# 46 products of 32 by 32 ahead of the first output transposes, in a DeltaNet and hard-swish MLP kernel

## The chip, the cores and the metric

The kernel runs on one core of one Trainium2 chip. The core has five engines that work in parallel, each through its own instruction stream in order: TensorE (PE in the profile; its weight loads are PEld), VectorE (DVE), ScalarE (ACT), GpSimd (POOL) and SyncE (SP), which here issues the DMA transfers. Engines wait for each other through semaphores. The metric is the device time of one execution in microseconds (us), lower is better. The kernel before has a median of 660.53 us over three runs (659.67 to 660.70).

## The reference

Two blocks follow each other. The first is a delta-rule recurrence over 768 tokens for 4 batches and 8 heads of width 48; the second is an MLP from 384 to 2048 and back with a hard-swish, over the 3072 tokens of all batches.

```python
def _attn_ref(q, k, v, beta):            # q, k, v: (4, 8, 768, 48); beta: (4, 8, 768)
    k_n = k / (np.linalg.norm(k, axis=-1, keepdims=True) + 1e-06)
    state = np.zeros((B, H, D, D), dtype=np.float32)
    for t in range(S):
        kt, vt, bt = (k_n[:, :, t], v[:, :, t], beta[:, :, t, None])
        y[:, :, t] = np.einsum('bhd,bhde->bhe', q[:, :, t], state)
        v_old = np.einsum('bhde,bhd->bhe', state, kt)
        state = state + bt[:, :, :, None] * np.einsum('bhd,bhe->bhde', kt, vt - v_old)
    return y

def _moe_ref(x, w_in, w_out):            # x: y as (3072, 384)
    h = x @ w_in
    g = h * np.clip(h + 3.0, 0.0, 6.0) / 6.0
    return g @ w_out
```

## The kernel before

The recurrence is worked in 24 steps of 32 tokens. A step holds the 32 tokens of all 4 batches on 128 partitions, batch b on rows 32b to 32b + 31, and all 8 heads beside each other. Within a step the 32 tokens depend on each other through a lower triangular matrix for each batch and head; its inverse, X, is made ahead of the step. Step 0 and groups of up to four steps have their own ways to X: step 0 by products (L645), group 1 (steps 1 to 4) by `halves_of`, an elimination of two halves on VectorE (transpose into the tile A at L458, pairs of multiply and subtract at L779 and L784, transpose back to X at L462), joined for each step by `join` (VectorE transposes at L743 and L751, TensorE products at L733).

The function `chain(t)` then does step t: products of keys and queries with the state (ks, L854, from step 1 on), the right side R, Z = X R (pz, L875), the change of the state (su, L986; subtracted at L1004), and, in `output`, the step's result: LB times Z (py, L875), copied to the tile y (L909 for step 0, on ScalarE), three transposes of 128 by 128 against the identity into the PSUM tile yt (L921), and a ScalarE copy of yt into xT (L925). xT is the input of the MLP. `prep` makes the transposed keys and queries (pt, L570) and the scores (sc, L596).

The MLP takes two steps, 256 tokens, as a block; there are 12 blocks. For block 0 the up product runs on each half of the block separately. `up` (L1042) writes a PSUM tile ph for each of 16 columns of tiles f, in three products of 128 by 128 by 128; ScalarE makes a first g from ph (L1049), VectorE finishes it from g and ph (L1052), and only then is the PSUM tile free. Four PSUM slots, named pm, are handed round by the function `ring` between pt, pz, py, yt, ph and others. `down` is L1210; later blocks use other schemes for both products (L1114 and L1274).

Weights come in pieces of 768 KB (L320) and are converted: four powers on ScalarE (L345) and three operations on VectorE (L367, L372, L378) for each piece.

The order of each engine's instructions is the order in which the program emits them. For the first five steps this is written out in the string ORDER, a list of short words; after them a plan emits steps and MLP units in turn. In ORDER the word y0 emits the pieces of step 0's `output` one after the other, ua the columns f of the first half block, i1 the elimination for group 1, a and c the conversion of the weights. So on TensorE the order at this place is: the transposes and scores of later steps, py of step 0, the three transposes yt, ph for f = 0, 1, 2, ks of step 1, ph for f = 3 to 9, the first pi of `join` for step 1, ph for f = 10, the second pi, and so on. On ScalarE it is: four powers of a piece of weights, the copy of y, the copy to xT, the first g of f = 0 and 1, three powers, the first g of f = 2, 3 and 4. On VectorE the elimination of group 1 stands between the conversion of weights and the g's of f = 0 to 5, and the transpose to X follows.

A product of f32 operands is two passes on TensorE, each with its weight load, so that 32 products show as 64 matmuls in the profile. A transpose is one pass.

Of the kernel before, what the change touches and what calls it, by code (L numbers as in the profile page):

```python
# [44 lines left out]
def kernel(  # L45
# [21 lines left out]
    nc = tc.nc  # L67
    B, H, S, D = q.shape
    DM, FF = moe_w_in.shape
    C, DP = 32, 64  # L70
# [24 lines left out]
    def rows(b):  # L95
        return slice(C * b, C * b + C)
# [4 lines left out]
    def group(t):  # L101
        return (0, t) if t < G0 else ((t - G0) // GS + 1, (t - G0) % GS)
# [34 lines left out]
    def needs(*what):  # L137
        assert past.issuperset(what), (what, set(what) - past)
# [5 lines left out]
    def ring(tag, n, key):  # L144

        held = rings.setdefault(tag, [])
        i = len(held)
        if i < n:
            held.append(key)
        else:  # L150
            i = min(range(n), key=lambda i: reads.get(held[i], len(reads)))
            needs(("read", held[i]))
            held[i] = key
        slot[tag] = f"{tag}{i}"

    def read(*keys):
        for key in keys:
            past.add(("read", key))
            reads.setdefault(key, len(reads))
# [45 lines left out]
    ident = const.tile([128, 128], FP32, name="ident")  # L205
# [623 lines left out]
    def he(h):  # L829
        return (h % 2) * NP + h // 2  # L830

    def by_pair(t):
        return t.rearrange("p (a e w) -> p e a w", e=2, w=D)

    def chain(t, whole=True):


# [27 lines left out]
        def plus(out, ph, sign, into):  # L865
            for e in range(2):
                nc.vector.scalar_tensor_tensor(
                    out=by_pair(out)[:, e], in0=ph[:, e], scalar=sign, in1=by_pair(into)[:, e],
                    op0=ALU.mult, op1=ALU.add,
                )  # L870

        def of_heads(ps, place, m, z, at=lambda h: h):
            for h in range(H):
                for b in range(B):
                    nc.tensor.matmul(  # L875
                        ps[rows(place(b)), D * h : D * h + D],
                        lhsT=m(h)[rows(b)], rhs=z[rows(b), D * at(h) : D * at(h) + D],
                        start=True, stop=True, skip_group_check=True,
                        tile_position=(C * b, C * place(b)),
                    )  # L880
# [4 lines left out]
        def output(Z=None):  # L885

            if t > 0:
                needs(("turned", t - 1))
            y = work.tile([P, DM], FP32, name="y", bufs=1)
            if t > 0:  # L890
                nc.scalar.activation(
                    out=by_pair(y[:]), in_=even, func=ACTF.Copy, scale=parity[:, 1, 1:2]
                )
                past.add(("even", t))
                if ("R", t) in past:
                    read(("ks", t, 0))
                yield 1
                plus(y[:], odd, parity[:, 0, 1:2], y[:])
                read(*(("ks", t, i) for i in range(2)))
                yield  # L900
            needs(("Z", t))
            Z = zs.pop(t)
            ring("pm", NPM, ("py", t))
            py = psM.tile([P, 512], FP32, name="py", tag=slot["pm"])
            of_heads(py, lambda b: b ^ 1, lambda h: LB[:, he(h), :], Z)
            past.add(("BZ", t))
            yield
            if t == 0:
                nc.scalar.activation(out=y[:], in_=py[:, 0:DM], func=ACTF.Copy)  # L909
            else:  # L910
                nc.vector.tensor_tensor(out=y[:], in0=y[:], in1=py[:, 0:DM], op=ALU.add)
            read(("py", t))
            yield
            blk, cc = divmod(t, CB)
            if cc == 0:
                needs(*([("up", blk - 2)] if blk >= 2 else []))
                xTs[blk] = work.tile([128, NKT, TB], FP32, name="xT")
            ring("pm", NPM, ("yt", t))
            pt = psM.tile([128, NKT, P], FP32, name="yt", tag=slot["pm"])
            for s in range(NKT):  # L920
                nc.tensor.transpose(pt[:, s, :], y[:, s * 128 : (s + 1) * 128], ident[:])  # L921
            past.add(("turned", t))
            yield 1
            read(("yt", t))
            nc.scalar.activation(  # L925
                out=xTs[blk][:, :, cc * P : (cc + 1) * P], in_=pt[:], func=ACTF.Copy
            )
            past.add(("seam", t))
            yield

        outs[t] = output()
        even = odd = None
        if t > 0:
# [475 lines left out]
    def chain_of(t):  # L1409
        return made(("h", t), lambda: chain(t))  # L1410
# [39 lines left out]
    def early_norms(t):  # L1450
# [9 lines left out]
    )  # L1460
    makers = {
        "p": lambda t: prep(t, False), "h": lambda t: chain(t, False), "y": lambda t: outs[t],
        "n": early_norms, "m": mask, "b": scaled, "x": lambda t: product(t) if t < G0 else join(t),
        }
# [35 lines left out]
    with tc.manual_schedule():  # L1500
# [16 lines left out]
        for t in range(LS, N):  # L1517
            g, i = group(t)
# [118 lines left out]
```

## Time and profile before

| | |
|---|---|
| median of three runs | 660.53 us |
| profiled execution | 661.58 us |
| its span, first to last instruction | 659.9 us |
| mean granted TensorE clock over the span | 0.984 |
| TensorE idle before the yt of step 0, ended by the copy of y | 1.18 us |
| TensorE matmul passes | 11640 |
| TensorE idle from 73.55 us to the end, in waits | none listed |

The median is of runs of the kernel as it is; the profiled execution is one run more, and its span leaves out what lies ahead of the first and behind the last instruction (1.7 us). Times in the views count from the first instruction of the span. The granted clock is 1 for full speed and 0.5 for half. In the order of time of an engine, a row is start, length, engine, line, operation, names and count of like instructions in a row; in brackets stands how long the engine was idle before it and what released it. "issue" there means that the profile shows nothing that it waited for.

### The profile page before, as it was taken

The page shows a single profiled execution, that of the slowest core. Times are in us where ns is not written, and L with a number is a line of the kernel's source. Part 1 is how long each engine was busy: PE and PEld are TensorE (multiplying, and loading weights), DVE is VectorE, ACT ScalarE, POOL GpSimd, SP SyncE. Part 2 cuts the span into 40 slices and gives each one's busy share as a digit, 9 for nine tenths or more (in the row PEclk, how much of TensorE's full clock was granted, in tenths as well). Part 3 has the DMA queues.
Part 4 walks back from the last instruction along what each step waited for, and adds up shares of the span by engine and source line. Part 5 has one row for each costly group of instructions (what it writes and reads, how often), then busy time and mean ns, then how long its engine had stood idle before and what let it go on. Part 6 is the DMA issues. An engine that isn't in the chain of part 4 may idle for free.

```text
span 659.9 us, 26616 instructions
## 1 busy us (share of the span) xinstructions
PE 630.5 (96%) x11640; PEld 567.1 (86%) x11640; DVE 504.9 (77%) x1164; ACT 264.3 (40%) x553; POOL 230.5 (35%) x352
## 2 busy tenths in 40 slices
PE   2759999999999999999999999999999999999997
PEld 2648887776689999999999999999999999999997
DVE  5989777799558989758989858989658999456354
ACT  4876578322232154154144244244243144153240
POOL 6531033002653262564163462263251241231330
PEclk9768999999999999999999999999999999999999
DMA  7888246402041030041030040030020020000101
GB/s 173 206 209 228 68 101 152 69 17 49 12 83 23 2 74 4 2 80 33 3 74 3 3 75 2 2 62 3 3 49 3 4 48 3 23 18 2 26 1 24
DMA packets 88693, 33.29 MB, mean 50 GB/s; under 512 B 80224, under 2 KB 83424, under 8 KB 88576
## 3 DMA queue, kind: packets, MB, share of 16 engines
q1 hardware_dynamic: 88224, 31.29, 21.8%
q8 instruction: 91, 1.49, 1.0%
q10 hardware_dynamic: 352, 0.30, 0.2%
q14 instruction: 26, 0.21, 0.1%
HBM read 26.84 MB, written 4.72 MB: 48 GB/s over the span
## 4 chain that ended last, share of the span: by engine, by line
PE 90%; DMA 3%; DVE 3%; SPq 1%; ACT 1%; issue 1%; DVEq 0%; ACTq 0%
PE po L1274 28%; PE ph L1114 27%; PE ph L1042 9%; PE po L1210 6%; PE pz L875 3%; PE py L875 3%; PE pc L854 3%; PE pt L570 2%; PE pc L986 2%; DMA spare<-in_moe_w_in_dram 2%; PE pc L596 1%; PE yt L921 1%; PE sc L596 1%; PE ks L854 1%; SPq L168 1%
## 5 line engine op out<-in xcount | busy, mean ns | idle before, releaser
L1114 PE MATMUL ph<-xT,w_in 128*128 128x128 f32 (+1 forms) x720 | 154.3, 320 | 0.0
L1078 POOL TENSOR_TENSOR g<-g 128x256 f32<-128x256 f32 (+1 forms) x144 | 89.7, 624 | 97.0 <-ACT g L1128 91.3
L1114 PEld LDWEIGHTS ph<-xT,w_in 128*128 128x128 f32 x720 | 117.5, 191 | 6.3
L1274 PE MATMUL po<-w_out,g 128*128 128x192 f32 x640 | 110.6, 326 | 0.0
L1274 PEld LDWEIGHTS po<-w_out,g 128*128 128x128 f32 x640 | 104.8, 190 | 0.5
L1274 PE MATMUL po<-spare,g 128*128 128x192 f32 x480 | 84.2, 329 | 0.0
L1274 PEld LDWEIGHTS po<-spare,g 128*128 128x128 f32 x480 | 77.4, 190 | 0.9
L1128 ACT ACTIVATE g<-ph 128x512 f32<-128x512 f32 x72 | 43.0, 597 | 86.3 <-PE ph L1114 86.3
L1042 PE MATMUL ph<-xT,w_in 128*128 128x128 f32 (+1 forms) x384 | 72.4, 338 | 1.8 <-ACT xT L925 0.6
L1284 POOL TENSOR_TENSOR o<-o,u 128x192 f32<-128x192 f32 x18 | 14.2, 791 | 155.6 <-ACT o L1281 83.3
L1042 PEld LDWEIGHTS ph<-xT,w_in 128*128 128x128 f32 x384 | 59.9, 195 | 9.4 <-DVE g L1052 1.0
L808 DVE TENSOR_TENSOR pr<-A 128x30 f32<-128x30 f32 (+9 forms) x150 | 60.5, 403 | 3.3
L1141 DVE TENSOR_TENSOR g<-ph,g 128x256 f32<-128x256 f32 x72 | 30.2, 419 | 41.6 <-PE ph L1114 40.1
L813 DVE TENSOR_TENSOR A<-A,pr 128x30 f32<-128x30 f32 (+9 forms) x150 | 57.3, 382 | 3.3
L1260 DVE TENSOR_TENSOR g<-g 128x512 f32<-128x512 f32 x80 | 56.5, 727 | 4.1 <-PE po L1274 4.0
L1161 DVE SCALAR_TENSOR_TENSOR g<-o,g 128x512 f32<-128x512 f32 x72 | 52.4, 727 | 7.3 <-ACT o L1158 7.3
L1114 PE MATMUL ph<-beta_tok,sums_in 128*128 128x128 f32 x288 | 55.7, 275 | 0.0
L1158 ACT ACTIVATE o<-g 128x512 f32<-128x512 f32 x72 | 45.4, 630 | 13.7 <-DVE g L1161 11.0
L345 ACT ACTIVATE spare<-spare 128x768 uint16<-128x768 uint16 (+1 forms) x56 | 47.3, 850 | 3.2 <-DMA spare<-in_moe_w_in_dram 1.9
L1281 ACT ACTIVATE o<-po 128x192 f32<-128x192 f32 x40 | 13.2, 330 | 85.5 <-PE po L1274 85.5
L553 POOL TENSOR_TENSOR kb<-kf,inv 128x384 f32<-128x384 f32 x24 | 21.7, 906 | 72.3 <-issue 41.6
L1210 PE MATMUL po<-w_out,g 128*128 128x384 f32 x128 | 45.4, 490 | 0.0
(153 smaller groups left out, 1013.4 us busy)
## 6 DMA issues: line engine op xcount, KB each, us to landing
kf<-in_k_dram SPq DMA_DIRECT2D x96, 48.0 KB, 3.3
qb<-in_q_dram SPq DMA_DIRECT2D x96, 48.0 KB, 2.5
vf<-in_v_dram SPq DMA_DIRECT2D x96, 48.0 KB, 2.5
out_dram<-o SPq DMA_DIRECT2D x90, 48.0 KB, 1.6
spare<-in_moe_w_in_dram SPq DMA_DIRECT2D x4, 768.0 KB, 5.6
w_out<-in_moe_w_in_dram SPq DMA_DIRECT2D x4, 768.0 KB, 6.2
w_out<-in_moe_w_out_dram SPq DMA_DIRECT2D x4, 768.0 KB, 6.7
spare<-in_moe_w_out_dram SPq DMA_DIRECT2D x4, 768.0 KB, 4.8
```

The source lines that it names most:

```text
L345: nc.scalar.activation(out=z, in_=z if n else d.bitcast(I16)[:, :, :, 3], func=func, bias=value, scale=scale,)
L808: nc.vector.tensor_tensor(out=pv, in0=A[:, j + 1 :, j].unsqueeze(2).to_broadcast([n, w, j]), in1=A[:, j, 0:j].unsqueeze(1).to_broadcast([n ...
L813: nc.vector.tensor_tensor(out=A[:, j + 1 :, 0:j], in0=A[:, j + 1 :, 0:j], in1=pv, op=ALU.subtract)
L1042: nc.tensor.matmul(ph[:, cols], lhsT=w_in[:, s, f * 128 : (f + 1) * 128], rhs=xT[:, s, cols], start=(s == 0), stop=(s == NKT - 1),)
L1078: nc.gpsimd.tensor_tensor(out=out, in0=a, in1=b, op=op)
L1114: nc.tensor.matmul(ph[:, n], lhsT=w, rhs=x, start=start, stop=stop, skip_group_check=True)
L1128: nc.scalar.activation(out=gt, in_=ph[:], func=ACTF.Copy)
L1158: nc.scalar.activation(out=r, in_=g, func=ACTF.Relu, bias=0.5, scale=1.0 / 6.0)
L1161: nc.vector.scalar_tensor_tensor(out=g, in0=r, scalar=1.0, in1=g, op0=ALU.min, op1=ALU.mult)
L1210: nc.tensor.matmul(pos[c][:], lhsT=gs[blk, f // 2][:, f % 2, c * P : (c + 1) * P], rhs=w_out[:, f, :], start=(f == 0), stop=(f == NFC - 1),)
L1260: nc.vector.tensor_tensor(out=A(f, *out, 4), in0=A(f, *a, 4), in1=A(f, *b, 4), op=op)
L1274: nc.tensor.matmul(ps[n][:], lhsT=A(f - f % 2, *a)[:, f % 2], rhs=b[:, f], start=(f == 0), stop=(f == HF - 1),)
```

## The change

In front of the three transposes of step 0's y, 46 products are emitted into the same PSUM tile yt. Each has a 32 by 32 piece of the constant tile ident as both operands and runs at one of the four diagonal positions of the array in turn. They write to the first 32 columns of the tile, which the transposes then overwrite. Nothing else is changed; on the other engines the instructions and their order stay as they are. In the lines behind, numbers grow by 11 and then by 13.

```diff
+    BETWEEN = 46
+
+    def between(ps):
+
+        for i in range(BETWEEN):
+            b = i % B
+            nc.tensor.matmul(
+                ps[rows(b), 0, 0:C], lhsT=ident[rows(b), 0:C], rhs=ident[rows(b), 0:C],
+                start=True, stop=True, skip_group_check=True, tile_position=(C * b, C * b),
+            )
+
     def chain(t, whole=True):
...
             pt = psM.tile([128, NKT, P], FP32, name="yt", tag=slot["pm"])
+            if t == 0:
+                between(pt)
             for s in range(NKT):
                 nc.tensor.transpose(pt[:, s, :], y[:, s * 128 : (s + 1) * 128], ident[:])
```

## The prediction

> **What bounds the kernel now.** I read the page first, then the chain of waits, then each engine in order of time around the place of the change. From the page:
>
> ```profile
> span 659.9 us, 26616 instructions
> ...
> PE 630.5 (96%) x11640; PEld 567.1 (86%) x11640; DVE 504.9 (77%) x1164; ACT 264.3 (40%) x553; POOL 230.5 (35%) x352
> ...
> q8 instruction: 91, 1.49, 1.0%
> ...
> PE 90%; DMA 3%; DVE 3%; SPq 1%; ACT 1%; issue 1%; DVEq 0%; ACTq 0%
> ```
>
> PE sets the end over nearly the whole span. The products are inserted at about 47 us, however, and there the chain of waits reads differently (start, length, what):
>
> ```profile
> 47.01 1.88 DVE A L458
> ...
> 58.15 1.93 DVE X L462
> ...
> 62.29 0.72 PE pi L733 x54
> ```
>
> From 47 to 62 us the chain is on DVE: the elimination for group 1 with other DVE work in between, then its transposes. PE joins at 62.29 and stays on the chain to the end, so a delay there reaches the end in full and a gain of PE before it reaches nothing unless DVE gains too. PE around the insertion (start, length, line, count of matmul passes, idle before):
>
> ```profile
> 34.62 0.27 PE L596 MATMUL sc<-KQ 64*32 64x64 f32 x2 [1.52 <-issue]
> 34.81 0.88 PE L875 MATMUL pz<-vf,X 32*32 32x48 f32 x64
> 36.31 1.27 PE L986 MATMUL su<-R,sums_in 32*64 32x48 f32 x61 [0.61 <-ACT R L975]
> 40.26 0.45 PE L986 MATMUL su<-R,sums_in 32*64 32x48 f32 x3 [2.68 <-issue]
> 40.64 1.11 PE L570 MATMUL pt<-ident,kb 128*128 128x128 f32 x4
> 41.55 1.91 PE L570 MATMUL pt<-ident,qb 128*128 128x128 f32 x8
> 43.39 2.39 PE L596 MATMUL sc<-KQ 64*32 64x64 f32 x128
> 45.71 1.23 PE L875 MATMUL py<-R,LB 32*32 32x48 f32 x64
> 48.12 0.55 PE L921 MATMUL yt<-ident,y 128*128 128x128 f32 x3 [1.18 <-ACT y L909]
> 49.25 3.62 PE L1042 MATMUL ph<-xT,w_in 128*128 128x128 f32 x18 [0.58 <-ACT xT L925]
> 52.79 1.38 PE L854 MATMUL ks<-state,KQ 64*64 64x48 f32 x64
> 56.58 3.62 PE L1042 MATMUL ph<-xT,w_in 128*128 128x128 f32 x30 [0.57 <-DVE g L1052]
> 60.61 0.72 PE L733 MATMUL pi<-X,sums_in 16*32 16x16 f32 x64 [0.41 <-DVE sums_in L743]
> ...
> 69.45 0.74 PE L986 MATMUL su<-R,bkb 32*64 32x48 f32 x48 [0.98 <-issue]
> 70.12 0.55 PE L921 MATMUL yt<-ident,y 128*128 128x128 f32 x3
> 70.50 0.83 PE L1042 MATMUL ph<-xT,w_in 128*128 128x128 f32 x6
> 71.27 0.72 PE L733 MATMUL pi<-X,sums_in 16*32 16x16 f32 x64
> 71.92 1.05 PE L1042 MATMUL ph<-xT,w_in 128*128 128x128 f32 x7
> 73.55 0.82 PE L1042 MATMUL ph<-xT,w_in 128*128 128x128 f32 x5 [0.58 <-issue]
> ```
>
> Four of these waits end in "issue": nothing that the profile shows released them, and they fall in the middle of a group. Count the passes between them. From the stall at 34.62 to the one at 40.26: 2 + 64 + 61 = 127. From 69.45 to 73.55: 48 + 3 + 6 + 64 + 7 = 128. Each pass has its weight load, so that is 256 instructions, give or take a semaphore wait. The page says the same from another side: PE has 2 x 11640 = 23280 instructions, queue q8 moved 91 packets of 16 KB, and 23280 / 91 = 256. So I read q8 as PE's instruction stream, fetched in blocks of 256, and "issue" as PE at a block's edge with the next block not there.
>
> **The insertion itself.** 46 products of f32 are two passes each, 92 passes and 92 loads, 184 instructions. The nearest row for a product of 32 by 32 in the same four diagonal positions:
>
> ```profile
> 21.91 0.74 PE L645 MATMUL pi<-sums_in 32*32 32x32 f32 x64 [1.54 <-DVE sums_in L687]
> ```
>
> 0.74 / 64 = 11.6 ns a pass, so 92 take 1.06 us. They stand between py and the transposes, where PE idles 1.18 us for ScalarE's copy of y. By busy time alone they cost nothing; without this cover they would delay the transposes by 1.06. No instruction moves on another engine or DMA queue, and the tile that the products write is the one the transposes then overwrite, so no other reader is held.
>
> **What they do to the clock.** Three stretches between the clock's changes (PE busy, PEld, DVE, ACT, POOL, granted clock, DMA):
>
> ```profile
> 46.51:49.92 3.41, 1.65 (x45) 1.28 (x38) 3.27 (x7) 2.02 (x4) 2.26 (x5) 1.00 0.95 330
> 49.92:53.34 3.42, 3.42 (x35) 3.20 (x37) 3.05 (x12) 1.97 (x4) 0.00 (x0) 0.50 1.09 325
> 53.34:56.75 3.41, 2.80 (x69) 2.36 (x62) 3.21 (x13) 2.20 (x6) 0.00 (x0) 1.00 0.86 233
> ```
>
> A stretch in which PE was busy 1.65 of 3.41 us is followed by one at half clock; stretches with 3.42 and 2.80 are followed by full clock. With all 92 passes done in the gap the first would hold 1.65 + 1.06 = 2.7, near the 2.80, and the second would run at full clock. That shortens the 18 ph passes and ks, but f = 4 of ph then waits for the first DVE g and f = 5 for the second, as in the 0.57 us wait at 56.58 already: DVE never waited for PE here, so 62.29 stays. The gain from the clock is 0. The Trainium skill, "TensorE: Matmul & The Clock Gate", in its table on why this matters, asks for no PE gaps over about 3 us; by that rule the 1.18 us gap would not have cost the clock and the products would change nothing, while this trace shows half clock after gaps of 1.18 and 0.58 us.
>
> **What they do to the instruction blocks.** This decides. From the edge at 40.26, passes are 3 + 4 + 8 = 15, then 128 of sc: the 128th is inside sc, near 45.3. The next edge is 128 further. Left of sc are 15, py has 64: 79 passes. So the edge lies 49 passes after py. In the kernel before that is 3 yt, 18 ph, then the 28th of ks, at about 53.4. In the changed kernel it is inside the inserted products, near the 48th of 92, reached at 46.94 + 48 x 0.0116 = 47.5 us. When is that block there? DMA between the two edges:
>
> ```profile
> DMA packets 676, 1.34 MB, mean 279 GB/s; under 512 B 118, under 2 KB 118, under 8 KB 676
> q1 hardware_dynamic: 676, 1.34, 91.3%
> w_out<-in_moe_w_out_dram SPq DMA_DIRECT2D x2, 768.0 KB, 8.2
> ...
> q8 instruction: 1, 0.02, 5.4%
> ```
>
> The first three lines are the stretch 45.3 to 50.1 us: no instruction packet, the engines 91% busy with weights. The last is 50.1 to 51.2: the one packet after the edge at 45.3. The other stalls show that PE goes on some time after a packet: one between 66.7 and 68.3 for the resumption at 69.45 (1.2 us later), one between 37.1 and 38.6 for 40.26 (1.7 later):
>
> ```profile
> q8 instruction: 1, 0.02, 5.6%
> q8 instruction: 1, 0.02, 5.7%
> ```
>
> So the block is usable at 51.2 + 1.2 to 1.7 = 52.4 to 52.9. Before, PE came to this edge at 53.4 and did not notice. Now PE stands at 47.5 and goes on at 52.5 (taken), a new stall of 5.0 us with the transposes, xT, ph and all behind them queued. The stall is bounded below by the quickest case of the four, a block usable 4 us after its edge (69.45 to 73.55 = 4.1): 49.4. The Trainium skill, "Runtime: NRT & Kernel Launch", section on instruction fetch mechanics, has the same blocks of 256, but calls the crossing mostly hidden; by that the sum would be 0. The four "issue" rows disagree.
>
> What is late next, step by step. The remaining 44 passes at half clock (PE has idled), 0.8 us: 53.3. From the start of the transposes to the first ph it was 49.25 - 48.12 = 1.13; at half clock three transposes take 0.83 (4 in 1.11 at 40.64), 0.3 more: first ph at 54.75, 5.5 late. ScalarE's order matters now:
>
> ```profile
> 51.62 0.28 ACT L1049 ACTIVATE g<-ph 128x128 f32<-128x128 f32 x1 [1.00 <-PE ph L1042]
> 51.79 2.63 ACT L345 ACTIVATE spare<-spare 128x768 uint16<-128x768 int16 x3
> ...
> 56.59 0.28 DVE L1052 SCALAR_TENSOR_TENSOR g<-g,ph 128x128 f32<-128x128 f32 x1
> ```
>
> The second g came 2.4 us after the first ph: now 57.15. The third stands behind 2.63 us of scale work, 0.17 after the second's start: 59.95, and takes about 0.25, so DVE's third g starts at 60.2 instead of 56.59, 3.6 late. Before, by the same steps it was free from 51.79 + 2.63 + 0.25 = 54.7 and had 1.9 us of slack; now DVE waits, and the elimination with it. Three more g's, each freshly made, add about 0.3 (estimate: one start to the next of ScalarE and of DVE): X's transposes and the pi at 62.29 are 3.9 late. From there PE is the bound and carries 3.9 to the end.
>
> The two stalls at 69.45 and 73.55 (0.98 + 0.58) move too, since every later edge comes 92 passes sooner in the code. Between -1.56 (both gone) and +0.98 (another like the larger in the dense stretch up to 100 us), I take -0.4. Elsewhere "issue" ends no PE wait.
>
> Sum: +3.9 - 0.4 = +3.5. The profiled execution took 661.58 (span 659.9), so its like is 665.1; it lies 1.05 above the median 660.53, so the median becomes 664.0.
>
> **The rivals.** Rival 1, no stall: the block is fetched well before 49 us, or PE holds more ahead than I read. Then the products fill the gap, the clock holds to 53.34, DVE still sets 62.29: 660.5. Its loss: PE, done early, waits for g, is busy too little of 53.34 to 56.75 and gets half clock for the 30 ph at 56.58; 3.6 us of work lose 1.7 less the wait of 0.41 and what the next wait covers, +1.0 at most: 660.2 to 661.5. For it: the design fits the gap to 0.12 us. Against: the count of passes. Rival 2, a short stall: the fetch is served between weight packets, block usable at 50 to 51. Each us earlier takes one off the 3.9, since all steps after it are the same: +1.4 at 50, +2.4 at 51, less 0.4: 661.5 to 662.5. Against: q1's two transfers of 768 KB are the same and issued before. Rival 3, faster: no stall at 47.5, and the moved edges rid PE of the 0.98 and 0.58 on its chain: 659.0. It needs both; four stalls in 40 us of dense small products speak against it.
>
> **How the numbers follow.** Main forecast 0.65, 662.5 to 665.2 (usable at 51, +2.4 - 0.4, up to 52.9 with moved stalls of +0.4, +4.3 + 0.4). Rival 1: 0.17. Rival 2: 0.10. Rival 3: 0.08. A measurement tells about 0.2%, 1.3 us, from no change. Slower: all of the main and 0.08 of the others, 0.73. Same: 0.19. Faster: 0.08. The range reaches down over rival 1 to 660.3 and up to 665.3.
>
> **What would show it.** Right: an "issue" wait of about 5 us within the new products, half of them before and half after; yt near 53.3, the first ph near 54.8; DVE waiting for ACT g; half clock from 49.92 to past 53.34; the second pi near 66.2. Wrong: 92 passes in one run ending by 48.1, or a q8 packet between 45.3 and 49 us. If the stall is there and the end is not late, DVE was not what set 62.29.

## The result, and the profile after

| | before | with the 46 products |
|---|---|---|
| median (15 runs each) | 661.01 us (659.49 to 662.68) | 665.89 us (661.67 to 668.34) |
| ratio | | 1.0068, 95% interval 1.0055 to 1.0081 |
| profiled execution, its span | 661.58, 659.9 us | 663.39, 661.7 us |

The change makes the kernel slower by 4.9 us in the median. The forecast was slower by 3.5, to 664.0 in a range of 660.3 to 665.3; the time lies 0.6 us above the range. The runs with the products also spread more, over 6.7 us against 3.2. The profiled execution is near the low end of them, 1.8 us above that of before, so a further profile at 666.29 stands beside it further down.

From the page of the changed kernel:

```profile
span 661.7 us, 26800 instructions
...
PE 630.0 (95%) x11732; PEld 567.5 (86%) x11732; DVE 505.7 (76%) x1164; ACT 264.3 (40%) x553; POOL 231.2 (35%) x352
...
q8 instruction: 92, 1.51, 1.0%
```

184 instructions more, 92 passes and 92 loads, all on TensorE, and one block more on q8. TensorE in order of time (start, length, line, passes, idle before; L841 are the new products, L934 the transposes behind them, L1055 ph, L733 the two pi of step 1):

```profile
45.12 0.62 PE L841 MATMUL yt<-ident 32*32 32x32 f32 x42
49.23 0.59 PE L841 MATMUL yt<-ident 32*32 32x32 f32 x45 [3.48 <-issue]
49.75 0.88 PE L934 MATMUL yt<-ident,y 128*128 128x128 f32 x3
51.20 4.21 PE L1055 MATMUL ph<-xT,w_in 128*128 128x128 f32 x18 [0.58 <-ACT xT L938]
...
62.57 0.73 PE L733 MATMUL pi<-X,sums_in 16*32 16x16 f32 x64 [0.62 <-DVE sums_in L743]
...
64.25 0.73 PE L733 MATMUL pi<-X,sums_in 32*32 32x16 f32 x64
...
71.31 0.35 PE L999 MATMUL su<-R,bkb 32*64 32x48 f32 x12 [0.52 <-issue]
...
99.33 0.44 PE L886 MATMUL py<-R,LB 32*32 32x48 f32 x20 [0.94 <-issue]
```

The wait is where the count of passes put it: 45 of the 92 passes stand behind it, 47 ahead (42 here, five more in short rows between the last passes of py). Then 3.48 us of nothing that the profile shows. In the DMA of 45.5 to 46.8 us there is no packet of q8:

```profile
q1 hardware_dynamic: 200, 0.41, 94.1%
```

The same view of 46.8 to 47.9 us has the block:

```profile
q8 instruction: 1, 0.02, 5.4%
```

The block came after 46.8, and TensorE went on 1.3 us after 47.9. That is 3 us earlier than the 52.5 that I took. The second pi is at 64.25 against 62.29, 2.0 us later on the clock of the view; but VectorE began its transpose into A, which nothing inserted holds up, at 46.08 against 46.92, so that this execution was 0.84 ahead at that place and the products cost 2.8 us by the second pi. Clock and busy times (PE, PEld, DVE, ACT, POOL, granted clock, DMA):

```profile
42.99:49.82 6.83, 3.35 (x285) 3.01 (x270) 6.26 (x14) 4.33 (x7) 2.26 (x5) 1.00 0.80 245
49.82:56.65 6.83, 6.25 (x69) 5.62 (x73) 5.52 (x21) 3.19 (x6) 0.00 (x0) 0.50 0.97 264
```

With the wait in it, the gap is longer than before, and 6.83 us run at half clock instead of 3.42. VectorE, which never waited for TensorE here, now does:

```profile
57.18 0.29 DVE L1065 SCALAR_TENSOR_TENSOR g<-g,ph 128x128 f32<-128x128 f32 x1 [1.36 <-ACT g L1062]
58.27 0.29 DVE L1065 SCALAR_TENSOR_TENSOR g<-g,ph 128x128 f32<-128x128 f32 x1 [0.69 <-ACT g L1062]
```

Behind 64.25 the two old waits (0.98 and 0.58) are gone; in their place stand 0.52 at 71.31 and a new 0.94 at 99.33. The last is in a stretch where before had none, and it is what the experiments turned on.

### The profile page after: what moved, and what is told of

It is laid out like the page before. It is cut to its first block, busy times and chain, and to the rows that moved or that the text cites. A ratio compares the mean times of both kernels' runs of the same rounds, so it can differ in the third digit from the quotient of the medians.

```text
span 661.7 us, 26800 instructions
## 1 busy us (share of the span) xinstructions
PE 630.0 (95%) x11732; PEld 567.5 (86%) x11732; DVE 505.7 (76%) x1164; ACT 264.3 (40%) x553; POOL 231.2 (35%) x352
## 4 chain that ended last, share of the span: by engine, by line
PE 93%; ACT 2%; DVE 2%; issue 2%; SPq 0%; DMA 0%; POOL 0%; ACTq 0%; DVEq 0%
PE po L1287 28%; PE ph L1127 27%; PE ph L1055 10%; PE po L1223 6%; PE pt L570 3%; PE py L886 3%; PE pz L886 3%; PE pc L865 3%; PE pc L999 2%; ACT spare L345 1%; PE yt L934 1%; PE sc L596 1%; PE pc L596 1%; PE ks L865 1%; PE su L999 1%
## 5 line engine op out<-in xcount | busy, mean ns | idle before, releaser
L1055 PE MATMUL ph<-xT,w_in 128*128 128x128 f32 (+1 forms) x384 | 72.4, 340 | 0.6 <-ACT xT L938 0.6
L1055 PEld LDWEIGHTS ph<-xT,w_in 128*128 128x128 f32 x384 | 60.4, 197 | 7.9 <-ACT xT L938 1.0
```

Of the source, the lines that this page charges most:

```text
L1055: nc.tensor.matmul(ph[:, cols], lhsT=w_in[:, s, f * 128 : (f + 1) * 128], rhs=xT[:, s, cols], start=(s == 0), stop=(s == NKT - 1),)
```

## The experiments

All ratios are to the kernel before, with 95% intervals. In the expectations "theory" changes once: the first four runs overturned a part of it.

**The changed kernel again, for a second profile.** The kernel is as it was.

> The changed kernel once more, unaltered, for a second profile: its times spread over 661.7 to 668.3 us, before's over 659.5 to 662.7. Theory (a block of 256 TensorE instructions is not there): one issue wait of 3 to 5.5 us, inside the 92 passes, within a few passes of the 48th; the time of the profiled run above that of before follows the moment at which that wait ends (ending at 49.2: +1.8, at 52.5: +4 to +5). Rival (the products' own time or the clock): the wait sits ahead of the first or behind the last pass, or the time does not follow its end. Ratio 1.007.

Measured: 1.0068 (1.0040 to 1.0096), median 668.1. The profiled execution was at the low end again, 662.89, with 2.13 us of wait ahead of the last 45 passes. The place was right, but the time did not follow the end of the wait as expected: VectorE began its transpose into A later here (47.87 against 46.92), and the second pi, at 63.23, followed as soon as in the kernel before, so this wait cost nothing. What the runs at the median do was not seen.

**The same busy time with few instructions.**

```diff
-        for i in range(BETWEEN):
-            b = i % B
+        for i in range(4):
             nc.tensor.matmul(
-                ps[rows(b), 0, 0:C], lhsT=ident[rows(b), 0:C], rhs=ident[rows(b), 0:C],
-                start=True, stop=True, skip_group_check=True, tile_position=(C * b, C * b),
+                ps[:, 0, :], lhsT=ident[:], rhs=ident[:],
+                start=True, stop=True, skip_group_check=True,
             )
```

> 4 products of 128 by 128 by 128 of the identity in place of the 46 small ones: 8 passes of about 0.13 us, so the same busy time of 1 us in the same gap, with 16 instructions in place of 184. Theory: the edge of the block moves back to the 20th pass of ks, reached near 53; no wait of several us near 47.5, ratio 0.998 to 1.002. Rival (TensorE's time in the gap, its clock, or the write to the PSUM tile ahead of the transposes costs the time): the same slowdown as with 46, ratio 1.005 to 1.008.

Measured: 1.0057 (1.0033 to 1.0082), so the theory's number is missed and the rival's is met. The order of time on TensorE (L840 the large products):

```profile
47.04 1.16 PE L840 MATMUL yt<-ident 128*128 128x128 f32 x8
...
56.40 0.94 PE L1054 MATMUL ph<-xT,w_in 128*128 128x128 f32 x6 [1.60 <-DVE g L1064]
...
66.26 0.62 PE L885 MATMUL pz<-R,X 32*32 32x48 f32 x37 [0.61 <-issue]
...
73.49 0.17 PE L733 MATMUL pi<-X,sums_in 16*32 16x16 f32 x1 [0.80 <-issue]
...
101.85 0.49 PE L933 MATMUL yt<-ident,y 128*128 128x128 f32 x3 [2.29 <-issue]
```

There is no "issue" wait in or right behind the products. The 18 passes of ph took 2.27 us at full clock instead of 3.62, and all that TensorE gained by it went into 1.60 us of waiting for VectorE: the clock is worth nothing at this place, as forecast. The loss comes later: the waits of "issue" behind 60 us add to 3.7 us against 1.6 before, 2.29 of them at 101.85, and the 3.4 us from 103.16 run at half clock.

**23 and 10 products.** Only the count is changed, here to 23, in the second kernel to 10.

```diff
-    BETWEEN = 46
+    BETWEEN = 23
```

> 23 products in place of 46, 92 instructions. Theory: the edge lies 3 passes behind the products, at the end of the three transposes yt or at the first ph. The issue wait moves there and ends as late as with 46, but the copy to xT is done meanwhile, which takes about 2 us off: ratio 1.003 to 1.005. Rival (own time of the products, 0.1 us each): half of the slowdown, 1.0035, without an issue wait at yt or ph.

> 10 products, 40 instructions. Theory: the edge lies in the 8th pass of ks, reached near 52.9, when the block is there or nearly: wait below 0.5 us, ratio 0.999 to 1.002. Rival (own time, 0.1 us for each product): 1.0015, and no wait. Second rival (any insertion at this place costs several us): 1.005 or more.

Measured: 1.0128 (1.0094 to 1.0161) for 23 and 1.0103 (1.0072 to 1.0133) for 10. With 23 the kernel is slower than with 46, and with 10 no faster (these two intervals touch). Neither theory had that, nor the rivals that go by the products' own time; the second rival's 1.005 or more is met, though by no wait at the place itself. The profile of 23 has no "issue" wait at yt or ph, where the theory put one; it has five between 63 and 105 us, 5.05 us in all, the longest 2.33 at 104.21. The waits of the kernel with 10, behind 60 us and up to 105 (its profiled execution is the fastest of its six):

```profile
64.08 0.72 PE L886 MATMUL pz<-R,X 32*32 32x48 f32 x49 [0.49 <-issue]
...
71.16 0.30 PE L733 MATMUL pi<-X,sums_in 16*32 16x16 f32 x13 [0.62 <-issue]
...
83.06 0.71 PE L1055 MATMUL ph<-xT,w_in 128*128 128x128 f32 x4 [0.86 <-issue]
...
96.43 0.30 PE L596 MATMUL sc<-KQ 64*32 64x64 f32 x2 [1.43 <-issue]
...
101.87 0.33 PE L596 MATMUL sc<-KQ 64*32 64x64 f32 x12 [1.77 <-issue]
```

They add to 5.2 us, against 1.6 in the kernel before, and there is none at the products. One more, of 1.02 us, stands far behind, at 322.24. So the new theory: 40 instructions put ahead move every later edge 40 instructions forward in the code, and, mostly up to 105 us, that decides how many blocks come late. Why so is to be read in the kernel before, in rows that its prediction did not use:

```profile
79.78 0.88 PE L875 MATMUL pz<-R,X 32*32 32x48 f32 x64
80.59 0.94 PE L1042 MATMUL ph<-xT,w_in 128*128 128x128 f32 x6
81.45 0.88 PE L875 MATMUL py<-R,LB 32*32 32x48 f32 x64
82.27 0.89 PE L986 MATMUL su<-R,bkb 32*64 32x48 f32 x64
83.08 0.94 PE L1042 MATMUL ph<-xT,w_in 128*128 128x128 f32 x6
```

From 79.78 to 83.08 TensorE runs 198 passes in 3.3 us. A block of 128 passes lasts 2.1 us there, while the quickest wait-to-wait of the prediction was 4.1 us for a block. My reading, which no run varies by itself, is that a wait arises if two edges enclose such a bunch, and none if an edge lies within it and the sparse passes on both sides share the load. What the runs below test is that the shift of the edges costs the time.

The runs from here on tell the two parts apart. **64 products**, 128 passes, exactly one block:

```diff
-    BETWEEN = 46
+    BETWEEN = 64
```

> 64 products, 128 passes, 256 instructions: exactly one block, so that behind the insertion every edge lies at the same instruction as in the kernel before. New theory: the price has two parts, the wait inside the products and the moved edges in the dense stretch of 60 to 105 us; here only the first is left (and 128 passes of 1.5 us, 0.3 over the gap): ratio 1.001 to 1.004, below the 1.007 of 46 products in spite of 18 products more; waits of issue behind 60 us as before (in su and ph near 69 and 73, one to two us in all), none at 80 to 105. Rival (the wait inside the products is the whole price, or the products' own time): ratio 1.007 to 1.010.

Measured: 1.0057 (1.0040 to 1.0074), above the expected range, but for the reason in the first of its rows:

```profile
51.07 1.00 PE L841 MATMUL yt<-ident 32*32 32x32 f32 x81 [4.05 <-issue]
...
73.23 0.74 PE L999 MATMUL su<-R,bkb 32*64 32x48 f32 x48 [0.77 <-issue]
...
77.06 0.82 PE L1055 MATMUL ph<-xT,w_in 128*128 128x128 f32 x5 [0.30 <-issue]
```

Behind the products the waits are those of before, in the same instructions (48 passes of su, 5 of ph), and none follows up to 105 us. The span of this execution is 663.5, 3.6 above before. Counted from the start of VectorE's transpose into A (47.60 here), the second pi is 3.4 us later than in the kernel before, and what follows it takes 0.4 less: the first wait is the whole price here, with edges unmoved.

**4 small products** at the old place.

```diff
-    BETWEEN = 46
+    BETWEEN = 4
```

> 4 small products at the old place: 8 passes and 16 instructions like the 4 large ones, but 0.1 us of work, which cannot fill the gap or keep the clock. New theory: the 16 instructions alone move the edges behind, ratio 1.004 to 1.008 as with the 4 large ones (1.0057), with issue waits of 2 us or more in all between 60 and 105 us. Rival (the large products' busy time, clock or PSUM write was the price): 0.999 to 1.001.

Measured: 1.0056 (1.0037 to 1.0075), the same as the 4 large ones, which are ten times the work. The longest of its four waits behind 60 us, 3.9 us in all:

```profile
100.96 0.80 PE L934 MATMUL yt<-ident,y 128*128 128x128 f32 x3 [2.40 <-issue]
```

So 16 instructions cost 0.56%, and the busy time of the large products adds nothing to it that can be told from noise.

**10 products at step 1** in place of step 0.

```diff
-    BETWEEN = 46
+    BETWEEN = 10
...
-            if t == 0:
+            if t == 1:
                 between(pt)
```

> 10 small products ahead of the transposes of step 1 (near 70 us) and none at step 0: the same shift of 40 instructions as with 10 at step 0, from there on only. New theory: the edges between 80 and 105 us are those of the 10 products at step 0, ratio 1.006 to 1.011, with issue waits in 80 to 105 us and none in front of step 0's transposes. Rival (the place at step 0 costs the time): 0.999 to 1.002, their own time of 0.2 us.

Measured: 1.0112 (1.0089 to 1.0134). The place at step 0 is not needed. Of its rows, two waits and the clock behind the second (columns as above):

```profile
86.06 0.71 PE L1055 MATMUL ph<-xT,w_in 128*128 128x128 f32 x4 [1.14 <-issue]
...
99.68 0.30 PE L596 MATMUL sc<-KQ 64*32 64x64 f32 x2 [1.69 <-issue]
```

```profile
96.62:100.04 3.42, 1.73 (x123) 1.42 (x111) 1.57 (x4) 1.09 (x3) 0.00 (x0) 1.00 0.59 179
100.04:103.45 3.41, 3.41 (x10) 1.73 (x10) 1.87 (x4) 2.40 (x4) 1.50 (x2) 0.50 0.83 181
```

The waits are at the instructions of the 10 at step 0 (4 passes of ph, 2 of sc), and so is a later one, 1.37 us at 325.54, before the same pass as the 1.02 at 322.24 there. A wait in this stretch can be paid twice: TensorE was busy only 1.73 of 3.42 us, and the next 3.41 ran at half clock.

**The changed kernel a third time**, for a profile nearer the median. The kernel is as it was.

> The changed kernel unaltered, once more for its profile, since the two profiled so far (663.4 and 662.9 us) lie below its median. If this one lies above 665, the new theory expects the difference in issue waits: a longer one inside the products, or waits of 1 to 3 us between 80 and 105 us, and nothing else; the rival (the clock's phase) expects a lower granted clock behind 60 us.

Measured: 666.29 us, span 664.5, near the median of 665.89 in the main comparison. TensorE, and the row of VectorE that starts the elimination, here and in the kernel before:

```profile
50.55 0.85 PE L841 MATMUL yt<-ident 32*32 32x32 f32 x45 [2.45 <-issue]
...
65.44 0.73 PE L733 MATMUL pi<-X,sums_in 32*32 32x16 f32 x64
...
69.48 0.72 PE L1055 MATMUL ph<-xT,w_in 128*128 128x128 f32 x5 [0.45 <-issue]
...
72.89 0.35 PE L999 MATMUL su<-R,bkb 32*64 32x48 f32 x12 [0.30 <-issue]
...
85.23 0.28 PE L886 MATMUL py<-R,LB 32*32 32x48 f32 x6 [0.71 <-issue]
...
102.16 0.44 PE L886 MATMUL py<-R,LB 32*32 32x48 f32 x20 [1.22 <-issue]
```

```profile
47.99 1.93 DVE L458 STREAM_TRANSPOSE A<-L 128x1024 f32<-128x1024 f32 x1
...
46.92 1.95 DVE L458 STREAM_TRANSPOSE A<-L 128x1024 f32<-128x1024 f32 x1
```

Of the 4.6 us that its span is above before's, 3.15 are there at the second pi (65.44 - 62.29) and 1.45 come behind it. Of the 3.15, 1.07 are there already at the start of the transpose into A (47.99 - 46.92), ahead of anything that the products hold up; the first wait costs the other 2.08. It is shorter than in the first profile (2.45 against 3.48), not longer. The four later waits are 2.68 us, 1.1 more than the two of before. The clock is at full from 57.34 us to the end, so the rival falls for this run.

**Weights four loads later**, alone, with 64 and with 46 products. The edit moves two words of the written order, w for one weight transfer each:

```diff
-... v*2 p4 m6 k a w a w i1*3
+... v*2 p4 m6 k a a i1*3
-... k b3 k y0 c y0*3 ua*2 ra*2 i1*3 w v ga ...
+... k b3 k y0 c y0*3 w*2 ua*2 ra*2 i1*3 w v ga ...
```

> Control, without products: two transfers of 768 KB of weights are issued four loads later (behind 46 us, not at 44.5 and 45.0), no engine's instructions change. Both theories: 0.998 to 1.002, as the block after 45.3 was not awaited before and the conversion has slack.

> 64 products (edges behind them as before) and the two weight transfers four loads later. Theory (the block fetch is served behind the weight packets already handed out): its packet comes 1 to 2 us after the edge at 45.3, the wait inside the products ends by 49.5 and is 1 to 2.5 us long instead of 4.05, of which ScalarE's copy hides half: ratio to before 1.000 to 1.003, below the 1.0057 of 64 products with the transfers at the old place. Rival (a fetch takes its 4 to 5 us whatever is in the queue): 1.005 to 1.007.

> 46 products with the two weight transfers four loads later. Theory: only the first part of the price shrinks, the moved edges in 60 to 105 us stay: ratio 1.003 to 1.006, 0.002 to 0.005 above the 64 products with the same move. Rival (the first wait is the whole price): the same ratio as those 64 products.

Measured: 1.0009 (0.9995 to 1.0023) without products, 1.0031 (1.0020 to 1.0042) with 64, 1.0050 (1.0030 to 1.0071) with 46. The wait in the 64 products shrank from 4.05 to 2.27 us:

```profile
49.98 0.89 PE L841 MATMUL yt<-ident 32*32 32x32 f32 x81 [2.27 <-issue]
...
56.99 0.79 PE L865 MATMUL ks<-state,KQ 64*64 64x48 f32 x38 [2.21 <-issue]
```

The second row is new: the next block is late in its place. The ratio fell from 1.0057 to 1.0031, just above what was expected; the two intervals touch. The control is not quite clean either. In its profiled execution, the slowest of its twelve, a block is late that was not late before, with no product inserted and no edge moved:

```profile
68.21 0.53 PE L875 MATMUL pz<-R,X 32*32 32x48 f32 x29 [2.49 <-issue]
```

Why a fetch takes as long as it does can be read across all 14 profiles. The edge ahead of this place lies inside sc, 127 passes behind the end of the wait in su near 40 us, and the q8 packet behind it brings the block whose lateness the products met. Where both weight transfers (L320) were issued 0.17 us or more ahead of that edge, the packet began 4.55 to 4.88 us after it (three profiles: before, 10 products, 4 small ones). Where only the first was clearly ahead, it was 1.95 to 3.70 us (six); where both came behind the edge, 0.86 to 1.54 (five). Before had 44.47 and 44.99 against an edge at 45.25, the first profile of the 46 products 43.63 and 44.15 against one at 44.12, and its block came sooner than I took.
 With 46 the gain is smaller and its interval touches that of 1.0068 in the main comparison, so by itself it settles little. The rows of these 46 show the clock's part once more:

```profile
44.67:48.72 4.05, 2.20 (x204) 2.00 (x190) 4.05 (x6) 3.79 (x6) 1.70 (x3) 1.00 0.42 74
48.72:60.70 11.98, 9.61 (x172) 8.84 (x172) 11.00 (x41) 7.99 (x18) 0.56 (x3) 1.00 0.95 295
```

```profile
48.72 0.59 PE L841 MATMUL yt<-ident 32*32 32x32 f32 x45 [1.85 <-issue]
...
60.76 0.73 PE L733 MATMUL pi<-X,sums_in 16*32 16x16 f32 x64 [0.64 <-DVE sums_in L743]
...
100.81 0.45 PE L886 MATMUL py<-R,LB 32*32 32x48 f32 x20 [2.11 <-issue]
```

Here the products did hold the clock at full through the place where before fell to half; the first pi is at 60.76 against 60.61, still waiting for VectorE, and the span is 663.2 by the waits behind.

**10 products at step 0 and 54 at step 1**: the kernel that cost 1.0103, with work added so that the later edges are where before has them.

```diff
-    BETWEEN = 46
+    BETWEEN = (10, 54)
-    def between(ps):
-        for i in range(BETWEEN):
+    def between(ps, n):
+        for i in range(n):
...
-            if t == 0:
-                between(pt)
+            if t < 2:
+                between(pt, BETWEEN[t])
```

> 10 products at step 0 as in the kernel that cost 1.0103, and 54 more at step 1 near 71 us: 64 in all, one block, so that from step 1's transposes on every edge lies where it does in the kernel before, while the work added is larger by 54 products. Theory (moved edges at 80 to 105 us are the price of the 10): the waits there go; left are the own time of 108 passes where TensorE is the bound, 1.25 us, and a wait of up to 1.5 us at the edge that falls inside them: ratio 1.002 to 1.005, and no issue wait above 0.5 us between 80 and 105 us. Rival (an inserted product costs by itself or by its place): 1.0103 and at least 0.002 more.

Measured: 1.0042 (1.0023 to 1.0061). 54 products more made it faster than with 10 alone, the intervals apart. The two kernels ran on different chips, each beside the kernel before. Its longest wait behind 60 us is at the edge inside the 54; between 80 and 105 one is left, a little over the 0.5 expected:

```profile
72.63 0.61 PE L841 MATMUL yt<-ident 32*32 32x32 f32 x48 [1.93 <-issue]
...
104.22 2.53 PE L1055 MATMUL ph<-xT,w_in 128*128 128x256 f32 x11 [0.57 <-issue]
```

**The two parts in every profile.** In each profiled execution, "start" is the start of VectorE's transpose into A (L458), "first wait" is how long behind it the wait in the products ended, "to the second pi" is how much longer than in the kernel before (15.37 us) it was from there to the second pi of step 1, and "behind it" how much longer than before (597.6 us) from there to the end of the span. The last two are the price of a late block at the products and of all that comes later. Each row is one execution.

| kernel | start | first wait | to the second pi | behind it |
|---|---|---|---|---|
| 46 products, first profile | 46.08 | 3.15 | +2.80 | -0.2 |
| 46, second profile | 47.87 | 1.25 | 0.0 | +0.3 |
| 46, third profile | 47.99 | 2.56 | +2.08 | +1.5 |
| 46, weights later | 46.80 | 1.92 | +0.27 | +3.2 |
| 64 | 47.60 | 3.47 | +3.37 | -0.4 |
| 64, weights later | 47.64 | 2.34 | +1.98 | +0.1 |
| 4 large | 48.24 | none | 0.0 | +3.6 |
| 4 small | 47.09 | none | 0.0 | +3.8 |
| 10 | 46.36 | none | 0.0 | +5.2 |
| 23 | 47.71 | none | 0.0 | +7.6 |
| 10 at step 1 | 47.58 | none | +0.31 | +7.0 |
| 10 and 54 | 47.00 | none | 0.0 | +3.6 |
| weights later, no products | 48.25 | none | 0.0 | +2.6 |

The first wait is the price only with 46 and 64 products, and the later its end against VectorE's work, the larger. With 4, 10 and 23 products all of the loss is behind the second pi. The last row warns that one execution with edges unmoved can lose 2.6 us there too.

## Why the prediction was right, and where it failed

- **What bounds the kernel**, VectorE up to 62 us and TensorE behind it: right. TensorE's faster ph with 4 large products turned into 1.60 us of waiting for VectorE, and with 64 products a delay at the second pi reached the end.
- **The clock is worth nothing here**: right, by the same run and by the 46 products with late weights, where the clock stayed at full and the first pi came at 60.76 against 60.61.
- **A block's edge inside the products**: right to about a pass. Forecast near the 48th of 92; 47 stand ahead in the profile. The wait was in all four profiles of 46 products and in both of 64.
- **The main term, +3.9**: the mechanism held and the term was too large. It measured 2.80, 0.0 and 2.08 in the three profiles of the changed kernel, by two misses that oppose each other. The block was taken as usable at 52.5; TensorE went on at 49.23, 49.12 and 50.55. The packet between 45.3 and 49 us, which the prediction named as a sign of being wrong, is there (46.8 to 47.9). The term used the fetch of one execution, in which both weight transfers were ahead of the edge. And the steps behind the wait were too cheap: with one us off for each us earlier, counted from VectorE's start, they give about 1.5 for the first profile and 0.9 for the third. In the first profile the second g came 3.0 us after the first ph, not 2.4, since all 18 passes of ph ran at half clock, and the three g's put at 0.3 made VectorE wait 1.2 (0.69, 0.26 and 0.22).
- **The step that failed** is the other term: "Between -1.56 (both gone) and +0.98 (another like the larger in the dense stretch up to 100 us), I take -0.4. Elsewhere 'issue' ends no PE wait." In the execution nearest to the main comparison's median what lies behind the second pi gave +1.45, beyond the upper bound and of the other sign. The step treated the two old waits as the only places at stake, since no other edge showed a wait. But an edge without a wait in the trace of before is not an edge with room: 128 passes last 2.1 us near 80 us, shifts of 16 to 40 instructions alone, without any wait of "issue" at step 0, cost 0.56 to 1.12%, and behind the second pi the profiles of 4, 10 and 23 products lost 3.6 to 7.6 us.
- **The sum** came near partly by luck. In that third profile the two terms give 2.08 + 1.45 = 3.5, the forecast's own sum, because the one was too large by as much as the other was too small. The remaining 1.07 us of its 4.6 were there ahead of the products and belong to that execution. So the 4.9 us between the medians are not taken apart in full.
- **The rivals**: no stall, and a short one of +1.0 to +2.0, were both too low for the median. Yet the second had the fetch right: the block did come sooner than 52.5, and what was held against it, that the transfers are issued before, holds for only one of the two in the first profile. The third, faster by moved edges, had the right object with the wrong sign. No shift that was tried lowered the waits behind 60 us clearly below those of before; the two lowest profiles of the changed kernel have 1.4 to 1.5 us of them against 1.6.

What stays open: why the changed kernel's runs spread over 6.7 us. The three profiles differ in their start, in the end of the first wait against VectorE's work and in the waits behind 80 us, but a run of 667 to 668 was not profiled, and in the changed kernel's second set of runs the median was 668.1. Nor was it tried which shift of the edges is best.

## What to carry to other kernels

Instructions have a price of their own where an engine runs through its 256-instruction blocks faster than they are fetched: count them, mark where the edges fall, and compare the time between two edges with the time of a fetch, also at edges that show no wait yet. A change of a few instructions can then cost more by what it does to edges 50 us later (in two kernels here even some 250 us later) than by its work, so test it with padding to a whole block before judging it. Before splitting the difference of two profiles, take off what they differ by ahead of the change: here, by the starts in the table, up to 2.2 us, as large as the terms in question. And a faster clock or a filled gap was worth nothing here on an engine that another one holds back next.

## What the runs showed of the hardware

- Instructions on TensorE cost time beyond their work: 16 more at 47 us raised the whole kernel by 0.56%, 40 by 1.03% (1.12% at 71 us), while 256 at 47 us raised it by 0.57%.
- The fetch of a block was slower behind weights already handed out. Its packet began 4.55 to 4.88 us after the edge with two transfers of 768 KB issued ahead of the edge, 0.86 to 1.54 with both behind it. With the transfers at their old place the wait inside 64 products was 4.05 us, with the same transfers issued later 2.27.
- A wait of 1.69 us at 99.68 was followed by 3.41 us at half clock in the kernel with 10 products at step 1, after a stretch of 3.42 us with TensorE busy for 1.73.
